# A linear-attention and squared-ReLU kernel: aligned tiles, a spread of u by a product, quarter products and a new order on every engine

## The chip, the cores and the metric

One core of a Trainium2 chip. The metric is the device time of one launch in microseconds; three runs of the kernel before gave 188.7, 190.06 and 193.52, with the median 190.06.

## The reference

Stage one is a linear attention with a per-channel decay w and a bonus u for the current token (batch 4, 8 heads, 768 tokens, 48 channels per head). Stage two is a feed-forward network with a squared ReLU on all 3072 tokens (384 to 2048 to 384).

```
state = 0                                   # per batch and head, 48 x 48
for t in range(768):
    cur  = outer(u * k[t], v[t])
    y[t] = r[t] @ (state + cur)
    state = w[t][:, None] * state + outer(k[t], v[t])
x = y with heads side by side               # 3072 x 384
out = maximum(x @ w_in, 0)**2 @ w_out
```

## The kernel before

The 3072 tokens are cut into twelve steps of 256, three to a batch. A step has two chunks c of 64 token pairs; the pair's two tokens are j = 0 and 1, so 128 partitions hold 128 pairs. One step s runs through these operations:

- `ld.s.w`, `.r`, `.k`, `.v` (L161): 384 KB each from HBM, descriptors of 384 bytes. The tiles of r and k have a third place per head, for the product with w.
- `ww_` (L243) multiplies the w of a pair, `lw_` (L247) takes the logarithm, `cum_` (L284 to L287) sums it over a chunk by products with triangular matrices, `exp_` and `ac_` (L291, L298) take the exponential. `rw_` and `kw_` (L256, L260) multiply r and k by w; `rd_` (L305) multiplies r and k by the decays into `rdec`.
- `tr_` with `rkt_`, or `dtr_` by DMA, transpose `rdec`. `p_` (L341) forms the scores in products of 64 rows by 64 columns of the array, four quarters of which work at once; `pm_` (L351, L354) masks them.
- `ku_`, `qp_`, `q_`, `vq_` (L264 to L277) form the bonus: u, k and r multiplied, summed over a head, times v.
- `su_` (L371) forms the change of the state, `ts_` and `sn_` (L381, L386) the next state S.
- `y_`, `yq_`, `yc_` (all recorded at L394) add up in one PSUM tile: masked scores times v, the bonus, and S. `ysb_`, `yt_`, `xt_` (L436, L444, L449), or `dyt_` by DMA, give xT.
- `m1_` (L464, eight per step, six products each) multiplies by w_in, `rl_` (L473 on ACT, L475 on DVE) applies the ReLU, `sq_` (L481, L483) squares, `m2_` (L489, eight per step, four products each) multiplies by w_out, `os_` (L496, L498) scales, `store` writes.

The weights come in eight blocks of 768 KB (`ld.g.i`, `ld.g.o`) and are cast to bf16 (`cast`, L184). `warm_` (L506) issues products of zeros that nothing uses.

Nothing is scheduled by a loop: the string `ORDER` lists every operation of the program, with the engine (`=A` ACT, `=V` DVE, `=G` POOL) and the PSUM place (`:0`, `:1`) where there is a choice, and a loop over its words issues them. Each engine runs its instructions in that order, and a load waits in the one queue of SP behind the loads and transposes before it. PSUM is split into two attention tiles of two banks (`att`), two banks for m1 (`m1_bank`) and two for m2 and the transposes (`bk`).

The bonus of a chunk has 64 rows (pairs) and must go to 128 output rows (both tokens j of a pair); `yq_` does that by a constant `spread` of 64 rows by 128 columns, zero in one half. u is brought to all 128 partitions by a load that reads its 1536 bytes 128 times (L189).

Of the kernel before, what the change touches and what calls it, by code (L numbers as in the profile page):

```python
# [17 lines left out]
ld.0.w warm_.16.0 ld.1.w ld.0.k ld.0.u ld.0.r ld.1.r ww_.1=V ww_.0=V ld.1.k ld.0.v lw_.0 lw_.1 kw_.0=V  # L18
cum_.1:0 ku_.0 cum_.0:1 ld.0.i warm_.13.0 ac_.0 ac_.1 rw_.0=V exp_.0 qp_.0 ld.1.v exp_.1 rd_.0.0 rd_.0.1
tr_.0.0:0 ld.1.i warm_.1.1 rw_.1=V ld.2.w rkt_.0.0=A tr_.0.1:1 q_.0 ku_.1 rkt_.0.1=A ld.3.i rd_.1.0  # L20
p_.0.0:mm v_.0=A kw_.1=V qp_.1 warm_.2.0 rd_.1.1 su_.0:1 ld.2.k tr_.1.0:0 pm_.0.0 ts_.0.0=A tr_.1.1:1
rkt_.1.0=A p_.0.1:0 sn_.0.0 ld.2.r pm_.0.1 rkt_.1.1=A vq_.0 v_.1=A ts_.0.1=V y_.0:0 q_.1 cast.i.0=A sn_.0.1
p_.1.1:mm yq_.0 pm_.1.1 yc_.0 vq_.1 p_.1.0:1 ysb_.0=A ld.2.i warm_.3.0 pm_.1.0 ld.0.o cast.i.1=A yt_.0:0
su_.1:0 xt_.0=V y_.1:1 ts_.1.0=V ld.1.o yq_.1 ww_.2=V m1_.0.2:0 sn_.1.0 m1_.0.3:1 rl_.0.2=A yc_.1 cast.i.3=V
rl_.0.3=A m1_.0.1:0 lw_.2 ts_.1.1=V ld.2.o ysb_.1=A m1_.0.6:1 sq_.0.1=V ld.2.v cum_.2:0 rl_.0.1=V rl_.0.6=A
yt_.1:1 exp_.2 m1_.0.7:1 xt_.1=V rw_.2=V m1_.0.0:0 rl_.0.7=A kw_.2=V rl_.0.0=A rd_.2.0 m1_.1.0:1 cast.i.2=G
ac_.2 m1_.1.7:0 sq_.0.3=A rl_.1.0=V tr_.2.0:0 rd_.2.1 ku_.2 ld.3.o rl_.1.7=A m1_.1.5:1 sq_.0.0=A ld.3.w
m1_.0.5:0 rl_.1.5=V ld.3.r tr_.2.1:1 cast.o.0=V sn_.1.1 rl_.0.5=A m1_.1.4:1 rkt_.2.0=V m1_.0.4:0 rl_.1.4=A
rkt_.2.1=A rl_.0.4=V qp_.2 m1_.1.1:1 sq_.1.2=V m2_.0.0.0:0 cast.o.1=A m1_.1.2:0 ld.3.k pp_.2:10 rl_.1.2=A
m2_.0.0.1 rl_.1.1=A pm_.2.1 v_.2=G sq_.0.2=A m1_.1.3:0 cast.o.2=G ld.3.v q_.2 m1_.1.6:1 m2_.0.1.0:1 pm_.2.0  # L30
rl_.1.6=A vq_.2 m2_.0.1.1 cast.o.3=A ld.4.w rl_.1.3=V su_.2:0 m2_.0.1.2 ww_.3=G sq_.1.0=A ld.4.r m2_.0.0.2
lw_.3 m2_.0.1.3 sq_.1.1=A cum_.3:1 os_.0.1=V ld.4.k m2_.0.0.3 rw_.3=V exp_.3 m2_.1.0.0:1 ts_.2.0=V kw_.3=G
sq_.1.3=A rd_.3.0 m2_.1.0.1 ld.5.r sn_.2.0 m2_.1.0.2 ac_.3 os_.0.0=A rd_.3.1 m2_.1.0.3 v_.3=A ku_.3
store.0.1 tr_.3.0:0 os_.1.0=V yy_.2:01 ww_.4=V qp_.3 ld.4.v rkt_.3.0=V lw_.4 tr_.3.1:1 ysb_.2=A m2_.1.1.0:0
rkt_.3.1=V ld.5.k ts_.3.0=A cum_.4:1 rw_.4=V sn_.3.0 yt_.2:1 exp_.4 m2_.1.1.1 xt_.2=V ac_.4 ld.5.w m2_.1.1.2
rd_.4.0 kw_.4=G m1_.2.1:1 ts_.3.1=V dtr_.4.0 ku_.4 m1_.2.0:0 rd_.4.1 rl_.2.1=A rl_.2.0=A m1_.2.5:1 q_.3
dtr_.4.1 pp_.3:01 sn_.3.1 rl_.2.5=A m1_.2.3:0 pm_.3.1 ld.6.w vq_.3 m2_.1.1.3 rl_.2.3=A pm_.3.0 m1_.2.2:1
v_.4=A qp_.4 m1_.2.6:0 ld.7.w sq_.2.0=A rl_.2.2=V yy_.3:10 rl_.2.6=V ld.5.v sq_.2.1=A ww_.5=V kw_.5=G
os_.1.1=A m1_.2.4:1 rw_.5=V ld.7.r ysb_.3=A m1_.2.7:0 lw_.5 yt_.3:1 ts_.4.0=V rl_.2.4=A m2_.2.0.0:0 ld.6.k
xt_.3=A sn_.4.0 sq_.2.2=V m2_.2.0.1 ku_.5 cum_.5:0 store.1.1 m2_.2.1.0:1 ac_.5 q_.4 exp_.5 m1_.3.1:1  # L40
ts_.4.1=V rl_.2.7=A m2_.2.1.1 rd_.5.0 rl_.3.1=A m1_.3.7:0 ww_.6=G sq_.2.3=A rd_.5.1 m2_.2.1.2 dtr_.5.0
sn_.4.1 rl_.3.7=A m1_.3.3:1 pp_.4:10 vq_.4 store.0.0 rl_.3.3=A m1_.3.2:0 dtr_.5.1 v_.5=A pm_.4.0 m1_.3.4:1
rl_.3.2=A ww_.7=G pm_.4.1 m2_.2.1.3 ld.6.r lw_.6 rl_.3.4=A qp_.5 m1_.3.0:0 ld.7.k lw_.7 kw_.6=V m2_.2.0.2
sq_.3.1=A ld.6.v yy_.4:10 ku_.6 ld.7.v rl_.3.0=V os_.2.1=V m2_.2.0.3 ysb_.4=A ts_.5.0=V store.1.0 sq_.3.0=V
m1_.3.5:1 sn_.5.0 yt_.4:1 rl_.3.5=A m1_.3.6:0 xt_.4=V sq_.3.2=A ld.8.w pp_.5:10 qp_.6 rl_.3.6=V m1_.4.0:1
os_.2.0=A pm_.5.0 sq_.3.3=A m2_.3.1.0:1 ld.8.r pm_.5.1 m1_.4.5:0 rw_.6=G rl_.4.0=A m2_.3.0.0:0 rw_.7=G q_.5
cum_.6:1 m1_.4.3:1 exp_.6 rl_.4.5=V kw_.7=G m2_.3.1.1 ac_.6 rd_.6.0 rl_.4.3=A cum_.7:0 vq_.5 m1_.4.1:0
exp_.7 rd_.6.1 dtr_.6.0 m2_.3.0.1 ac_.7 rd_.7.0 ww_.8=G v_.6=A m1_.4.2:1 dtr_.6.1 m2_.3.0.2 rd_.7.1
rl_.4.1=A v_.7=G rl_.4.2=A m2_.3.0.3 q_.6 sq_.4.0=A ld.8.k yy_.5:10 vq_.6 sq_.4.1=A m1_.4.4:0 ts_.6.0=A
dtr_.7.0 os_.3.0=A m1_.4.6:1 sn_.6.0 ysb_.5=A m2_.3.1.2 ld.9.r rl_.4.6=V ku_.7 lw_.8 yt_.5:0 store.2.0  # L50
rl_.4.4=A ts_.6.1=V m2_.3.1.3 xt_.5=V ld.9.w pp_.6:01 ld.9.k sn_.6.1 m1_.4.7:1 pm_.6.0 m1_.5.1:0 ku_.8
# [38 lines left out]
def kernel(  # L90
# [54 lines left out]
    def bf16_bank(i):  # L145
        return bk[int(i)][:].bitcast(BF16)
# [420 lines left out]
```

## Time and profile before

| | |
|---|---|
| Runs of the kernel before | 188.7, 190.06, 193.52 us |
| Span of the profiled execution, first to last instruction | 186.7 us |
| Its own total time | not on the page; the span is 2.0 under the fastest run, 3.4 under the median |
| Granted TensorE clock | 0.999 |
| Busy: PE, DVE, ACT, POOL | 177.0, 125.8, 125.1, 104.9 us |
| Chain that ended last | PE 80%, DVE 8%, ACT 5%, issue 3%, DMA 3% |
| DMA of the kernel | 35.46 MB, 82.5% of the sixteen engines' time |

How to read it. Busy time is the union of an engine's instructions. Idle time of an engine that is not the bound costs nothing. In the slices of the page a digit is the busy share in tenths of one fortieth of the span, 4.67 us. A timeline row gives start, length, engine, line, operation, output and inputs, the count of merged instructions, and in brackets the idle time before it with what ended it. A waits row gives the waiting engine and line, what it waited for, and total us, times and longest wait. A group row ends with the busy time, the mean ns of one, and the idle time before them. A chain row gives start, length and count. A row of the stretches gives the stretch, its length, busy time and count of an engine, the granted clock, the share of DMA engines busy and GB/s. PE's ends are modelled, so the time that a product costs is read from one start to the next.

### The profile page before, as it was taken

Reading aid. Unit: us, or ns where it says so; the run is one execution under the profiler, and the core shown is the slowest. Engines: PE = TensorE matmul, PEld = TensorE weight load, DVE = VectorE, ACT = ScalarE, POOL = GpSimd, SP = SyncE. Lnnn points to the kernel's source line nnn. Section 1 sums busy time; section 2 is a strip of 40 time slices with the busy share of each in tenths; the row PEclk is TensorE's granted clock in tenths of the full one; section 3 lists DMA queues with packets and bytes.
Section 4 is the critical chain, followed back from the end, with each engine's and each line's share of the span. In section 5 each row is a group of like instructions: output and inputs, shape, how many; then the busy total and the mean of one; then the engine's idle time right before and its main releaser. Section 6 shows DMA issues by size and latency. Waiting matters only on the chain.

```text
span 186.7 us, 5422 instructions
## 1 busy us (share of the span) xinstructions
PE 177.0 (95%) x2303; PEld 125.4 (67%) x2303; DVE 125.8 (67%) x170; ACT 125.1 (67%) x205; POOL 104.9 (56%) x99
## 2 busy tenths in 40 slices
PE   7686998999999999999999999999999999999992
PEld 2344587766777777777776766777666777776761
DVE  4379979686799876983849699795946472562020
ACT  5278978889659795797687577968541656156732
POOL 7289627695897998959496981563934130000000
PEclk9999999999999999999999999999999999999999
DMA  6999999999999999979999999890539150203022
GB/s 151 269 274 341 330 280 381 340 280 264 275 234 218 257 239 236 248 148 147 279 185 260 220 270 251 240 147 32 66 63 201 30 172 0 46 0 126 4 84 84
DMA packets 78952, 35.81 MB, mean 192 GB/s; under 512 B 72144, under 2 KB 77392, under 8 KB 78928
## 3 DMA queue, kind: packets, MB, share of 16 engines
q1 hardware_dynamic: 78928, 35.46, 82.5%
q8 instruction: 18, 0.29, 0.7%
q14 instruction: 6, 0.05, 0.1%
HBM read 25.36 MB, written 4.72 MB: 161 GB/s over the span
## 4 chain that ended last, share of the span: by engine, by line
PE 80%; DVE 8%; ACT 5%; issue 3%; DMA 3%; SPq 0%; ACTq 0%
PE m L464 32%; PE bk L489 31%; PE att L394 8%; DVE rdec_buf L305 4%; PE att L341 3%; PE att L371 3%; DMA w_raw<-in_w_dram 3%; PE bk L444 1%; PE att L286 1%; PE att L287 1%; ACT att L291 1%; DVE r_raw L256 1%; ACT ac_buf L298 1%; DVE pmT L351 1%; DVE pmT L354 1%
## 5 line engine op out<-in xcount | busy, mean ns | idle before, releaser
L464 PE MATMUL m<-xT,wi_sb 128*128 128x256 bf16 x576 | 74.3, 273 | 0.5 <-ACT gt L473 0.5
L489 PE MATMUL bk<-wo_sb,gt 128*128 128x384 bf16 x384 | 71.9, 326 | 0.0
L464 PEld LDWEIGHTS <-wi_sb 128*128 128x128 bf16 x576 | 54.9, 98 | 13.9 <-issue 1.4
L473 ACT ACTIVATE gt<-m 128x512 f16<-128x512 f32 x68 | 39.7, 596 | 34.4 <-PE m L464 34.1
L489 PEld LDWEIGHTS <-gt 128*128 128x128 bf16 x384 | 36.9, 98 | 19.3
L481 ACT ACTIVATE gt<-gt 128x1024 bf16<-128x1024 f16 x36 | 37.6, 1053 | 0.9 <-DVE gt L475 0.7
L354 DVE TENSOR_TENSOR pmT<-att,mask 128x1024 bf16<-128x1024 f32 x22 | 26.3, 1218 | 5.6 <-PE att L341 5.5
L386 POOL TENSOR_TENSOR S<-t_state,ac_buf 128x384 bf16<-128x384 f32 x20 | 18.7, 935 | 19.9 <-DVE t_state L381 13.2
L475 DVE TENSOR_SCALAR gt<-m 128x512 f16<-128x512 f32 x28 | 19.2, 687 | 14.6 <-PE m L464 11.9
L264 POOL TENSOR_TENSOR ku<-k_raw,u_bc 128x768 f32<-128x768 f32 x12 | 22.5, 1878 | 9.1 <-DVE q L273 4.7
L269 POOL TENSOR_TENSOR ku<-ku,r_raw 128x768 f32<-128x768 f32 x12 | 22.9, 1910 | 1.0 <-DMA r_raw<-in_r_dram 0.8
L277 POOL TENSOR_TENSOR vq<-v_raw,q 128x768 bf16<-128x768 f32 x12 | 18.2, 1520 | 9.1 <-DVE q L273 4.8
L305 DVE TENSOR_TENSOR rdec_buf<-r_raw,att 128x768 bf16<-128x768 f32 x12 | 11.3, 952 | 3.8 <-ACT att L291 2.2
L498 DVE TENSOR_SCALAR o_sb<-bk 128x384 f32<-128x384 f32 x11 | 6.1, 551 | 11.0 <-PE bk L489 11.0
L291 ACT ACTIVATE att<-att 128x768 f32<-128x768 f32 x12 | 9.4, 795 | 3.7 <-PE att L287 3.6
L305 DVE TENSOR_TENSOR rdec_buf<-k_raw,att 128x768 bf16<-128x768 f32 x12 | 11.4, 947 | 0.5 <-ACT ac_buf L298 0.5
L506 PE MATMUL bk<-warm 128*128 128x512 bf16 x35 | 10.5, 452 | 1.2 <-DVE half_ones L212 1.2
L273 DVE TENSOR_REDUCE q<-ku 128x16 f32<-128x768 f32 x12 | 11.3, 943 | 0.0
L496 ACT ACTIVATE o_sb<-bk 128x384 f32<-128x384 f32 x13 | 6.4, 490 | 6.2 <-PE bk L489 6.2
L483 DVE TENSOR_TENSOR gt<-gt 128x1024 bf16<-128x1024 f16 x12 | 8.9, 753 | 2.0 <-ACT gt L473 2.0
L381 DVE TENSOR_TENSOR t_state<-S,att 128x384 f32<-128x384 bf16 x16 | 8.7, 546 | 1.8 <-PE att L371 1.8
L247 ACT ACTIVATE lw_buf<-ww 128x384 bf16<-128x384 f32 x12 | 6.2, 524 | 5.3 <-DVE ww L243 5.3
(72 smaller groups left out, 179.8 us busy)
## 6 DMA issues: line engine op xcount, KB each, us to landing
w_raw<-in_w_dram SPq DMA_DIRECT2D x12, 384.0 KB, 5.1
k_raw<-in_k_dram SPq DMA_DIRECT2D x12, 384.0 KB, 6.1
r_raw<-in_r_dram SPq DMA_DIRECT2D x12, 384.0 KB, 6.2
v_raw<-in_v_dram SPq DMA_DIRECT2D x12, 384.0 KB, 6.0
out_dram<-o_sb SPq DMA_DIRECT2D x24, 192.0 KB, 3.1
w_st<-in_moe_w_in_dram SPq DMA_DIRECT2D x4, 768.0 KB, 8.5
w_st<-in_moe_w_out_dram SPq DMA_DIRECT2D x4, 768.0 KB, 8.7
rkT<-rdec_buf SPq DMA_TRANSPOSE x16, 4.0
```

The costliest lines, as they stand in the source:

```text
L264: nc.gpsimd.tensor_mul(ku[:], raw["k", s][:, :, 1:3, :], u_bc[:, :, None, :].to_broadcast([C, H, 2, D]))
L269: nc.gpsimd.tensor_mul(ku[:], ku[:], raw["r", s][:, :, 0:2, :])
L277: nc.gpsimd.tensor_mul(vq[:].rearrange("p j h d -> p h j d"), raw["v", s][:], tiles.pop(("q", s))[:, :, :, None].to_broadcast([C, H, 2, D]))
L305: nc.vector.tensor_mul(rdec[:, i, :, :, 0:D], x.rearrange("p h j d -> p j h d"), cs[:, i, 0:DM].rearrange("p (h d) -> p h d", h=H)[:, None ...
L354: nc.vector.tensor_mul(pmT, ps_p[:].rearrange("p e (a x) -> p (e a) x", a=2), mk.to_broadcast([C, 4, 2 * C]))
L386: nc.gpsimd.tensor_mul(t[:], tiles.pop(("ts", s, c))[:].rearrange("p (a e d) -> p a e d", a=HP, e=2), tiles["a_c", s][:, :, c, :, None].to ...
L394: nc.tensor.matmul(ps_y[rows, c, cols], lhsT, rhs, start=fresh, stop=True, skip_group_check=True)
L464: nc.tensor.matmul(ps1[:, j, :], wi_sb[:, n // 4, kk, n % 4 * 128:(n % 4 + 1) * 128], tiles["xT", s][:, :, kk, :], start=(kk == 0), stop=( ...
L473: nc.scalar.activation(rl, m1, AF.Relu, scale=RS)
L475: nc.vector.tensor_scalar(out=rl, in0=m1, scalar1=RS, scalar2=0.0, op0=ALU.mult, op1=ALU.max)
L481: nc.scalar.activation(gt, rl, AF.Square)
L489: nc.tensor.matmul(m2, gt[:, n, c * C:(c + 1) * C], wo_sb[:, n, :], start=(n == 0), stop=(n == NT - 1))
```

## The change

- Tiles: all buffers are allocated once, each a multiple of 128 bytes long, and handed out by a small allocator (`buf`). r and k get 160 elements of room per head instead of 144, with the place that a load writes on a multiple of 128 bytes. Output tiles reuse one weight buffer.
- PSUM: the four banks of m1, m2 and the transposes become one pool (`one`), any of which an operation may name.
- u: one row of 1536 bytes is loaded, an f32 product with a row of ones spreads it over the partitions (`ub_`), and ACT copies it out (`uc_`).
- The bonus: `spread` goes; `yq_` multiplies by 64 x 64 blocks of the identity into the two halves of the output rows, four products on four quarters of the array.
- The order: `pp_` and `yy_`, which kept p, and su, y, yq and yc, together, are taken apart, and the whole string is another one, with other engines for many operations. Casts of w_in: all four on ACT (two before). ReLU: 51 on ACT and 45 on DVE (68 and 28). Products ww, rw, kw: 25 on POOL and 11 on DVE (15 and 21). Dummy products: 24 (35). The number of m1, m2, attention operations and transposes by DMA is the same.

```diff
-ld.0.w warm_.16.0 ld.1.w ld.0.k ld.0.u ld.0.r ld.1.r ww_.1=V ww_.0=V ld.1.k ld.0.v lw_.0 lw_.1 kw_.0=V
-cum_.1:0 ku_.0 cum_.0:1 ld.0.i warm_.13.0 ac_.0 ac_.1 rw_.0=V exp_.0 qp_.0 ld.1.v exp_.1 rd_.0.0 rd_.0.1
...
+ld.0.w ww_.0=V ld.1.w ld.0.u ld.0.r ld.0.k ld.1.k rw_.0=G warm_.10.1 lw_.0 ww_.1=V lw_.1 kw_.0=V cum_.0:1 exp_.0 ac_.0
+rd_.0.0 ub_:1 uc_=A warm_.1.3 cum_.1:0 ld.1.r ld.0.v ld.0.i warm_.4.3 tr_.0.0:0 rd_.0.1 tr_.0.1:1 ku_.0 ac_.1 ld.1.v
+exp_.1 warm_.4.2 rkt_.0.0=A kw_.1=V rd_.1.1 ld.1.i ld.2.i rkt_.0.1=A v_.0=A rw_.1=G warm_.1.0 p_.0.0:n rd_.1.0 su_.0:1
+ld.3.i tr_.1.1:2 ts_.0.0=A qp_.0 sn_.0.0 ld.2.w ld.2.k pm_.0.0 q_.0 p_.0.1:0 vq_.0 ku_.1 warm_.4.0 pm_.0.1 tr_.1.0:3
+rkt_.1.0=V rkt_.1.1=A cast.i.0=A ld.2.r ld.2.v ld.0.o y_.0:0 yc_.0 yq_.0 v_.1=A ld.3.k ts_.0.1=V sn_.0.1 p_.1.1:n
+pm_.1.1 ysb_.0=A p_.1.0:1 yt_.0:3 xt_.0=V su_.1:0 m1_.0.1:3 qp_.1 ts_.1.0=V sn_.1.0 cast.i.1=A pm_.1.0 cast.i.2=A
...
+        w=(4, [C, H, 2, D], FP32), r=(4, [C, 1280], FP32), k=(4, [C, 1312], FP32), v=(4, [C, H, 2, D], FP32),
...
+    for kind, first in (("r", 0), ("k", 16)):
+        free[kind] = [t[:, first:first + H * 160].rearrange("p (h x) -> p h x", h=H)[:, :, 0:3 * D].rearrange(
+            "p h (n d) -> p h n d", n=3) for t in free[kind]]
...
     def load_u():
-        nc.sync.dma_start(
-            out=u_bc[:],
-            in_=bass.AP(tensor=u.tensor, offset=u.offset,
-                        ap=[[0, C]] + [list(x) for x in u.ap]))
+        nc.sync.dma_start(out=u_row[0:1, :],
+                          in_=bass.AP(tensor=u.tensor, offset=u.offset, ap=[[0, 1]] + [list(x) for x in u.ap]))
+
+    def ub_():
+        tiles["ub"] = one[int(slot["ub_",])]
+        nc.tensor.matmul(tiles["ub"][:, 0:DM], ones_row[0:1, :], u_row[0:1, :], start=True, stop=True)
+
+    def uc_():
+        copy = nc.scalar.copy if where["uc_",] == "A" else nc.vector.tensor_copy
+        copy(u_bc[:].rearrange("p h d -> p (h d)"), tiles["ub"][:, 0:DM])
...
     def yq_(s):
-        vq = tiles.pop(("vq", s))
-        for j in range(2):
-            for c in range(2):
-                part = slice(c * Q, (c + 1) * Q)
-                y_mm(s, c, slice(0, DM), spread[part, j], vq[part, j].rearrange("p h d -> p (h d)"))
+        vq = buf("vq", s)
+        for c in range(2):
+            part = slice(c * Q, (c + 1) * Q)
+            for j in range(2):
+                y_mm(s, c, slice(0, DM), ident[part, part], vq[part, j].rearrange("p h d -> p (h d)"), j)
...
-    def yy_(s):
-        if s + 1 < NS:
-            su_(s + 1)
-        y_(s)
-        yq_(s)
-        yc_(s)
```

More of the change, by code (lines that the diff above doesn't have):

```diff
@@ L23 @@
[L23 to L27, printed above, removed]
@@ new lines @@
+    att = [ps_pool.tile([C, 2, 512], FP32, name=f"att{i}") for i in range(2)]
+    one = [ps_pool.tile([C, 512], FP32, name=f"one{i}") for i in range(4)]
+    def bf16_bank(i):
+        return one[i][:].bitcast(BF16)
+    kinds = dict(
+        w=(4, [C, H, 2, D], FP32), r=(4, [C, 1280], FP32), k=(4, [C, 1312], FP32), v=(4, [C, H, 2, D], FP32),
+        w_st=(4, [C, 4 * DM], FP32), ww=(2, [C, H, D], FP32), v_bf=(3, [C, H, 2, D], BF16),
+        ku=(2, [C, H, 2, D], FP32), q=(3, [C, 32], FP32), vq=(2, [C, 2, H, D], BF16), vqt=(2, [C, 2, DM], BF16),
+        rkT=(2, [C, 2, 2, HP, C], BF16), pmT=(2, [C, 2, 4, 2, C], BF16), t=(2, [C, DM], FP32),
+        S=(6, [C, HP, 2, D], BF16), y_sb=(2, [C, 2, DM], BF16), xT=(4, [C, 2, KT, C], BF16),
+        gt=(3, [C, NT, T], BF16))
@@ new lines, with uses_of, buf @@
+    uses = dict(w=4, r=4, k=4, v=3, w_st=2, ww=2, v_bf=3, ku=3, q=2, vq=2, vqt=2, rkT=5, pmT=3, t=2, y_sb=2,
+                xT=9, gt=20, o=2)
+    live, done = {}, {}
+    def uses_of(kind, key):
+        if kind == "S":
+            s, c = key
+            return 2 if c and s % NB == NB - 1 else 3
+        return uses[kind]
+    def buf(kind, *key):
+        held = live.setdefault((kind,) + key, [])
+        if not held:
+            held += [free[kind].pop(0), uses_of(kind, key)]
+        held[1] -= 1
+        if not held[1]:
+            given = live.pop((kind,) + key)[0]
+            free[kind].append(given)
+            done[kind] = done.get(kind, 0) + 1
+            if kind == "w_st" and done[kind] == 5:
+                free["o"] += [given[:, i * DM:(i + 1) * DM] for i in range(4)]
+        return held[0]
@@ L199 @@
     ident = consts.tile([C, C], BF16)
-    spread = consts.tile([C, 2, C], BF16)
-    half_ones = consts.tile([C, 2], BF16)
+    half_ones = consts.tile([C, 64], BF16, name="half_ones")[:, 0:2]
     mask = consts.tile([C, 2, 2, Q], BF16)
@@ L256, in rw_ @@
-        mul(raw["r", s][:, :, 2, :], raw["r", s][:, :, 1, :], raw["w", s][:, :, 0, :])
+        r_raw, w_raw = buf("r", s), buf("w", s)
+        product("rw_", s)(r_raw[:, :, 2, :], r_raw[:, :, 1, :], w_raw[:, :, 0, :])
     def kw_(s):
-        mul = nc.gpsimd.tensor_mul if where["kw_", s] == "G" else nc.vector.tensor_mul
-        mul(raw["k", s][:, :, 0, :], raw["k", s][:, :, 1, :], raw["w", s][:, :, 1, :])
+        k_raw, w_raw = buf("k", s), buf("w", s)
+        product("kw_", s)(k_raw[:, :, 0, :], k_raw[:, :, 1, :], w_raw[:, :, 1, :])
@@ L400, in y_ @@
         tiles["y", s] = att[int(slot["y_", s])]
-        pmT, v_bf = tiles.pop(("pmT", s)), tiles["v", s]
+        pmT, v_bf = buf("pmT", s), buf("v_bf", s)
         for e in range(2):
@@ L535 @@
             where[(name,) + args] = engine
-            slot.update(zip(takes(name, *args), banks))
+            if bank:
+                slot[(name,) + args[:2]] = bank
             operations[name](*args)
```

315 lines of the change are left out of this document (142 added, 173 removed).

## The prediction

> **What bounds the kernel now.** I read the page's totals and slices first, then the waits, then the chain that ended last.
>
> ```profile
> span 186.7 us, 5422 instructions
> PE 177.0 (95%) x2303; PEld 125.4 (67%) x2303; DVE 125.8 (67%) x170; ACT 125.1 (67%) x205; POOL 104.9 (56%) x99
> PE   7686998999999999999999999999999999999992
> DMA  6999999999999999979999999890539150203022
> GB/s 151 269 274 341 330 280 381 340 280 264 275 234 218 257 239 236 248 148 147 279 185 260 220 270 251 240 147 32 66 63 201 30 172 0 46 0 126 4 84 84
> ```
>
> PE is full from the sixth slice (4.67 us each) to the last. The waits say who waits for whom:
>
> ```profile
> ACT gt L473 <- PE m L464: 34.1, 32, 4.0
> ...
> PE m L464 <- ACT gt L473: 0.5, 1, 0.5
> ```
>
> ACT's ReLUs wait 34.1 us for PE's products, PE waits 0.5 for the ReLUs. So the time is a prologue, then PE's own work, then a tail. The timeline of PE gives the prologue's end, the chain the tail:
>
> ```profile
> 1.19 5.73 PE L506 MATMUL bk<-warm 128*128 128x512 bf16 x16 [1.19 <-DVE half_ones L212]
> 9.20 2.97 PE L506 MATMUL bk<-warm 128*128 128x512 bf16 x13
> 14.70 0.42 PE L341 MATMUL m<-rkT 64*64 64x128 bf16 x16 [1.15 <-ACT rkT L323]
> 18.90 0.57 PE L394 MATMUL att<-v_bf,pmT 64*128 64x48 bf16 x32 [1.36 <-DVE pmT L354]
> 23.39 1.48 PE L464 MATMUL m<-xT,wi_sb 128*128 128x256 bf16 x12
> ...
> 177.50 5.86 PE bk L489 x36
> 183.39 0.49 ACT o_sb L496
> ```
>
> The first product with w_in starts at 23.4; PE ends at 183.4; the last scaling and store take 3.3. The 160 us between shrink only with PE's work or its waits. The page gives this execution's span, not its total: the three runs have a median of 190.06, 3.4 above the span, and a fastest of 188.7, 2.0 above. I make the sum on the span and carry the difference to the median.
>
> **The prologue.** Loads come from one queue, in order, so the next question is when each lands. The timelines of DVE and POOL show it, as the start of a job that waited for a load:
>
> ```profile
> 6.22 1.03 DVE L243 TENSOR_TENSOR ww<-w_raw 128x384 f32<-128x384 f32 x2 [2.59 <-DMA w_raw<-in_w_dram]
> 7.62 0.56 DVE L260 TENSOR_TENSOR k_raw<-k_raw,w_raw 128x384 f32<-128x384 f32 x1 [0.36 <-DMA k_raw<-in_k_dram]
> ...
> 11.05 0.95 DVE L305 TENSOR_TENSOR rdec_buf<-r_raw,att 128x768 bf16<-128x768 f32 x1 [0.34 <-ACT att L291]
> ...
> 16.44 1.28 DVE L351 TENSOR_TENSOR pmT<-m,mask 128x512 bf16<-128x512 f32 x2
> 17.64 1.21 DVE L354 TENSOR_TENSOR pmT<-att,mask 128x1024 bf16<-128x1024 f32 x1
> 13.20 1.82 POOL L264 TENSOR_TENSOR ku<-k_raw,u_bc 128x768 f32<-128x768 f32 x1 [0.81 <-DMA k_raw<-in_k_dram]
> ```
>
> From 6.2 (w of step 1) to 13.2 (k of step 1) four tensors of 384 KB and the 192 KB of u land: 7.0 us, about 1.5 per tensor. In the new order k of step 0 stands behind w, w, a u of one row and r, so it lands near 6.2 + 2 x 1.5 = 9.2. Then kw_ 0.56, and rd_0.0 starts at 9.8 where it started at 11.05. From rd_0.0 to the first score product took 3.65 (11.05 to 14.70): 13.45. DVE now does kw_1, rd_1.1 and rd_1.0 before the first mask product; r of step 1 lands at 12.2, its product on POOL ends at 13.2, rd_1.0 at 14.2. Then pm_0.0 1.28, q_0 0.94, pm_0.1 1.21: y_0 at 17.7 instead of 18.90. y_0 to yq_0 takes about 1.2 (18.9). ACT is free for the copy after v of step 1, which lands at 6.2 + 5 x 1.5 + 3.0 + 1.5 = 18.2 (one weight block is two tensors long) and takes 0.83: 19.0. The copy 0.8, the six transposes and their latency 0.55, the copy of xT 0.56 follow:
>
> ```profile
> 20.89 0.79 ACT L436 CAST y_sb<-att 128x768 bf16<-128x768 f32 x1
> 21.73 0.51 PE L444 MATMUL bk<-ident,y_sb 128*128 128x128 bf16 x6
> 22.42 0.55 DVE L449 COPY xT<-bk 128x768 bf16<-128x768 bf16 x1
> ```
>
> That gives a first product with w_in at 21.0: **-2.4 us**. Of before, 0.9 went because a cast of w_in stood ahead of this copy on ACT and three dummy products ahead of the transposes; both are moved. In exchange y_1 and its bonus, before the first product with w_in until now, come after it: **+0.8**.
>
> **Tiles at 128 bytes** have no row of their own: nothing here loads the same shape into an aligned and an unaligned place. Bounds: nothing, or all loads at the best slice's 381 GB/s instead of the 304 that slices 2 to 5 average, 20% of the 15 us of loads up to v of step 1: -3.0. Loads pace everything up to 21 us, and the addresses of all loaded tiles move, from 32 bytes past a multiple of 128 to 0; I take a third, **-1.0**. The one-row u takes 191 KB off the queue (already in the 9.2), and adds one f32 product and one copy of 128x384 on ACT (0.49, as the scaling at 183.39 above), in the time in which both wait for k.
>
> **The bonus on quarters.** The timeline of one step, and pieces of the chain:
>
> ```profile
> 135.73 0.49 PE L464 MATMUL m<-xT,wi_sb 128*128 128x256 bf16 x3
> 136.15 0.52 PE L371 MATMUL att<-v_bf,rdec_buf 64*128 64x96 bf16 x16
> 136.50 0.56 PE L394 MATMUL att<-v_bf,pmT 64*128 64x48 bf16 x32
> 136.91 0.48 PE L394 MATMUL att<-vq,spread 64*128 64x384 bf16 x4
> 137.32 0.36 PE L394 MATMUL att<-S,rkT 128*64 128x96 bf16 x8
> ...
> 52.44 1.31 PE m L464 x12
> ...
> 54.59 0.57 PE att L341 x32
> ...
> 55.92 0.65 PE bk L489 x4
> ```
>
> A product of 384 columns is 0.65/4 = 0.163. The four of the bonus take 0.41 (136.91 to 137.32): two pairs, 0.325, and 0.09 for changing the array from 64x128 to 128x64. The same 0.09 shows where L464 gives way to L371: 0.42 (135.73 to 136.15) for three of 1.31/12 = 0.109. Four quarters at once cost 0.163 at best; by the score products, where 32 quarters of 128 columns take 0.57 (some three at a time), 0.21. With the change behind them that is 0.25 to 0.30: 0.11 to 0.16 saved, over twelve steps 1.3 to 1.9. But the quarters are a fourth shape between two others, and su, y, yq and yc no longer stand together. Counted in the two programs, PE changes shape 67 times before and 81 after: 14 x 0.09 = 1.3 given back. Net **-0.3** (-0.9 if a change between two 64-row shapes costs nothing, +0.6 if it costs double).
>
> The Trainium skill (TensorEngine Tiling (Array Packing), Tiling Modes, Key Properties) says that changing the tiling mode drains TensorE while changing the tile alone doesn't; the 0.09 above agrees, and by that rule the quarters pay only where the shape before or after them is the same.
>
> **The orders.** ReLUs move from ACT (68 to 51) to DVE (28 to 45), and products with w from DVE (21 to 11) to POOL (15 to 25):
>
> ```profile
> L473 ACT ACTIVATE gt<-m 128x512 f16<-128x512 f32 x68 | 39.7, 596 | 34.4 <-PE m L464 34.1
> L475 DVE TENSOR_SCALAR gt<-m 128x512 f16<-128x512 f32 x28 | 19.2, 687 | 14.6 <-PE m L464 11.9 <-ACT gt L473 2.6
> L243 POOL TENSOR_TENSOR ww<-w_raw 128x384 f32<-128x384 f32 x5 | 5.0, 1007 | 0.6 <-DMA w_raw<-in_w_dram 0.6
> ```
>
> ACT loses 17 x 0.6 = 10 us, DVE gains 11.7 and loses about 10 products of 0.55 or more, POOL gains 10 x 1.0. All stay off the bound by the 34.1 and 11.9 in which they wait for PE; cover gone, POOL is the one with a price (below). The products with w_in get four banks in place of two, so the bank waits of PE (0.5 in the waits) should go: **-0.4**; other waits I take as many as before.
>
> **Sum:** -2.4 + 0.8 - 1.0 - 0.3 - 0.4 = -3.3: span 183.4, time 190.06 - 3.3 = 186.8, 1.7% less. (2% either way, 3.8 us, is about what a measurement of this kernel can tell from no change.)
>
> **Rivals.** *The lead is kept and the loads gain their full bound:* -1.0 becomes -3.0, time 184.8, faster by over 2%. For it: DMA is at 9 in every slice up to the 18th, and weights are still landing when PE begins. Against: only the prologue turns loads into time. With the better shape bound (-0.6 more) and a product with w_in at 20.5 it is 183.7; PE's work allows no less.
>
> *POOL becomes the bound of steps 3 and 4 (slower).* PE takes its queue in order, so yq_3 blocks all behind it until vq_3 is there. In the POOL and PE timelines and POOL's busy time by stage:
>
> ```profile
> 29.30 1.46 POOL L184 CAST wi_sb<-w_st 128x1536 bf16<-128x1536 f32 x1 [4.72 <-DMA w_st<-in_moe_w_in_dram]
> 55.39 1.48 POOL L277 TENSOR_TENSOR vq<-v_raw,q 128x768 bf16<-128x768 f32 x1 [0.24 <-PE att L341]
> 58.57 0.48 PE L394 MATMUL att<-vq,spread 64*128 64x384 bf16 x4
> 8.00:50.00 42.00, 30.31 (x21) 1.00 1.13 308
> ```
>
> vq_3 ends 1.7 us before PE wants it. After, seven more products of 1.0 stand ahead of it (the two casts remain, of other blocks), and PE comes about 2.4 sooner: POOL must win 7.0 + 2.4 - 1.7 = 7.7. It idled 11.7 of the 42 us from 8 to 50, of which 4.7 for one weight block that it no longer casts; so I expect it to win most. If it wins none, 186.8 + 7.7 = 194.5; it turns the sign once over 3.3 is lost, and passes 2% slower near 7.
>
> *Nothing is kept:* the products with w_in start sooner but stand waiting for casts or ReLUs, as ACT now casts all four blocks of w_in; the lead of 2.6 goes, time about 189.5.
>
> *The clock.* Dummy products fall from 35 to 24. The later thirteen took 2.97, 0.23 each; the first sixteen took 5.73, 2.1 more than at that rate: PE starts slow, although the granted clock reads 1.00. If it falls back once while it waits for loads, the real products lose as much: time 188.9. For: the first dummies stop near 5.5 now. Against: the thirteen at 9.20 were fast though the sixteen had ended at 6.92.
>
> The Trainium skill (TensorE: Matmul & The Clock Gate, Part 1) halves the clock after an idle window of about 3.4 us; no gap in the walk above is that long, so by that rule the clock stays.
>
> **How the numbers follow.** Forecast near 186.8 0.38; loads or quarters better, 183 to 186, 0.32; nothing kept or the clock, 188.5 to 192, 0.16; POOL, 192 to 196, 0.14. The forecast stands so close to 2% (186.3) that a third of it counts as faster: faster 0.32 + 0.13 = 0.45; slower takes the POOL case and 0.04 of the third, 0.18; within 2% 0.37. Range 182.8 to 192.0: below it lies PE's work, above it most of the POOL case.
>
> **What would show it.** Right: first product with w_in near 21 us, k of step 0 landed near 9 us; PE's end 158 to 160 us after that start; the bonus at 0.2 per step, with 0.09 ahead of it; POOL with little idle time from 30 to 65 us and no wait of PE for vq. Wrong: a first product at 23 or later, tensors still 1.5 us apart, or waits of PE for vq_3, casts or ReLUs of over 2 us together.

## The result, and the profile after

The changed kernel takes 183.08 us (median of four runs, 182.77 to 183.29), the kernel before 189.47 (188.7 to 193.52); the ratio is 0.968, with a 95% interval of 0.9635 to 0.9725. The profiled execution took 183.09, its span is 181.3. The forecast was 186.8, 1.7% faster; it is 3.2% faster, inside the range and 0.6 below the lowest time that the first rival allowed. One of the four runs before, 193.52, was a slow one: without it the median before is 188.88. So the 6.4 us between the medians is more than the change is worth: it is 5.8 without that run, 5.3 to 5.5 against the later sessions (188.41 to 188.6), and 5.4 by the spans of the two profiles (186.7 and 181.3).

The page of the changed kernel (totals and slices, here 4.53 us each), and its waits, in the form in which those of before were shown:

```profile
span 181.3 us, 5434 instructions
PE 174.1 (96%) x2293; PEld 125.1 (69%) x2294; DVE 127.1 (70%) x176; ACT 120.0 (66%) x191; POOL 110.8 (61%) x104
PE   7978899999999999999999999999999999999992
DMA  5999999998999599979999559983659821302023
...
ACT gt_b L481 <- PE one L474: 24.0, 17, 4.9
...
PE one L474 <- ACT gt_b L481: 0.5, 1, 0.5
```

PE is still the bound: its slices stand at 9 from the sixth to the last but one. The timeline of PE, and the last piece of the chain:

```profile
1.19 4.45 PE L513 MATMUL one<-warm 128*128 128x512 bf16 x10 [1.19 <-DVE warm L235]
15.86 0.57 PE L411 MATMUL att<-v_bf_b,pmT_b 64*128 64x48 bf16 x32 [0.29 <-DVE pmT_b L376]
17.96 0.51 PE L457 MATMUL one<-ident,y_sb_b 128*128 128x128 bf16 x6 [0.50 <-ACT y_sb_b L449]
19.12 2.78 PE L474 MATMUL one<-xT_b,wi_sb 128*128 128x256 bf16 x24 [0.20 <-DVE xT_b L461]
22.43 0.81 PE L474 MATMUL one<-xT_b,wi_sb 128*128 128x256 bf16 x6 [0.53 <-ACT gt_b L481]
...
168.90 9.11 PE one L497 x56
```

The first product with w_in starts at 19.12 (before 23.39): 4.3 sooner. PE ends at 178.0 (before 183.4). So 158.9 us lie between, 1.1 less than the 160 of before. The loads show why the start is early. DVE's and POOL's jobs that waited for a load:

```profile
4.23 0.56 DVE L267 TENSOR_TENSOR ww_b<-w_b 128x384 f32<-128x384 f32 x1 [0.48 <-DMA w_b<-in_w_dram]
5.44 0.56 DVE L267 TENSOR_TENSOR ww_b<-w_b 128x384 f32<-128x384 f32 x1 [0.66 <-DMA w_b<-in_w_dram]
7.89 0.56 DVE L283 TENSOR_TENSOR k_b<-k_b,w_b 128x384 f32<-128x384 f32 x1 [1.89 <-DMA k_b<-in_k_dram]
10.40 1.10 POOL L279 TENSOR_TENSOR r_b<-r_b,w_b 128x384 f32<-128x384 f32 x1 [0.24 <-DMA r_b<-in_r_dram]
```

From w of step 0 (4.2) to r of step 1 (10.4) lie five tensors (w, r, k, k, r): 1.2 us each, where before it was about 1.5. k of step 0 is there at 7.9; the prediction had 9.2.

### The profile page after: what moved, and what is told of

Read it like the earlier page. It is cut to its first block, busy times and chain, and to the rows that moved or that the text cites. A ratio compares the mean times of both kernels' runs of the same rounds, so it can differ in the third digit from the quotient of the medians.

```text
span 181.3 us, 5434 instructions
## 1 busy us (share of the span) xinstructions
PE 174.1 (96%) x2293; PEld 125.1 (69%) x2294; DVE 127.1 (70%) x176; ACT 120.0 (66%) x191; POOL 110.8 (61%) x104
## 4 chain that ended last, share of the span: by engine, by line
PE 86%; DMA 5%; SPq 5%; issue 1%; ACT 1%
PE one L497 35%; PE one L474 34%; PE att L411 7%; DMA w_st_b<-in_moe_w_in_dram 5%; SPq L180 3%; PE att L365 3%; PE att L387 2%; SPq L188 1%; PE one L341 1%; PE att L313 1%; PE one L457 1%; PE att L314 1%; SPq L208 1%; PE att L311 0%; ACT gt_b L481 0%
## 5 line engine op out<-in xcount | busy, mean ns | idle before, releaser
L474 PE MATMUL one<-xT_b,wi_sb 128*128 128x256 bf16 x576 | 71.2, 273 | 0.7 <-ACT gt_b L481 0.5
L497 PE MATMUL one<-wo_sb,gt_b 128*128 128x384 bf16 x384 | 68.9, 326 | 0.0
L497 PEld LDWEIGHTS <-gt_b 128*128 128x128 bf16 x384 | 36.7, 98 | 21.7 <-ACT gt_b L489 0.2
L481 ACT ACTIVATE gt_b<-one 128x512 f16<-128x512 f32 x51 | 29.9, 596 | 24.6 <-PE one L474 24.0
L483 DVE TENSOR_SCALAR gt_b<-one 128x512 f16<-128x512 f32 x45 | 30.3, 685 | 17.0 <-PE one L474 15.7
L489 ACT ACTIVATE gt_b<-gt_b 128x1024 bf16<-128x1024 f16 x38 | 39.4, 1054 | 0.9 <-DVE gt_b L483 0.7
L376 DVE TENSOR_TENSOR pmT_b<-att,mask 128x1024 bf16<-128x1024 f32 x22 | 26.0, 1216 | 6.2 <-PE att L365 6.2
L286 POOL TENSOR_TENSOR ku_b<-k_b,u_bc 128x768 f32<-128x768 f32 x12 | 22.8, 1910 | 3.0 <-DMA k_b<-in_k_dram 2.3
L291 POOL TENSOR_TENSOR ku_b<-ku_b,r_b 128x768 f32<-128x768 f32 x12 | 21.8, 1814 | 1.2 <-DMA r_b<-in_r_dram 1.2
L297 POOL TENSOR_TENSOR vq_b<-v_b,q_b 128x768 bf16<-128x768 f32 x12 | 18.1, 1506 | 0.4 <-DVE q_b L294 0.3
```

What stands on the lines that cost most here:

```text
L286: nc.gpsimd.tensor_mul(buf("ku", s)[:], buf("k", s)[:, :, 1:3, :], u_bc[:, :, None, :].to_broadcast([C, H, 2, D]))
L291: nc.gpsimd.tensor_mul(ku[:], ku[:], buf("r", s)[:, :, 0:2, :])
L297: nc.gpsimd.tensor_mul(buf("vq", s)[:].rearrange("p j h d -> p h j d"), buf("v", s)[:], buf("q", s)[:, :, :, None].to_broadcast([C, H, 2, D]))
L376: nc.vector.tensor_mul(pmT, ps_p[:].rearrange("p e (a x) -> p (e a) x", a=2), mk.to_broadcast([C, 4, 2 * C]))
L474: nc.tensor.matmul(ps1[:, j, :], wi_sb[:, n // 4, kk, n % 4 * 128:(n % 4 + 1) * 128], xT[:, :, kk, :], start=(kk == 0), stop=(kk == KT - 1))
L481: nc.scalar.activation(rl, m1, AF.Relu, scale=RS)
```

## The experiments

Fourteen kernels were run. Times are medians; the ratio is to the kernel before in the same session, whose median was 188.4 to 189.5. "The start" is that of the first product with w_in.

### One part taken out at a time

**All tiles off the 128 bytes** (e1): one small tile ahead of all others shifts every address by 32 bytes.

```diff
+    shift = consts.tile([C, 8], FP32, name="shift")
     free = {kind: [consts.tile(shape, dtype, name=f"{kind}_b{i}") for i in range(n)]
...
```

> The changed kernel with every tile moved by 32 bytes, so that no tile starts at a multiple of 128 (as before the change); all else the same. Theory A (the loads land faster at aligned places, and this is the gain that the forecast undersized): tensors of 384 KB land 1.4 to 1.5 us apart instead of 1.2, k of step 0 at 8.7 to 9.3 instead of 7.87, the first product with w_in at 20.5 to 21.3 instead of 19.12, time 184.6 to 185.5. Theory B (the gain over the forecast comes from the order): first product within 0.3 of 19.12, time 183.0 to 183.5.

It took 187.34, ratio 0.9916 (0.9882 to 0.9949): 4.3 more than the changed kernel, so most of the gain is gone. One row of DVE, then the stretches of PE (stretch, its length, busy time, count, granted clock, DMA share, GB/s) and two of its waits, in this kernel:

```profile
8.93 0.56 DVE L284 TENSOR_TENSOR k_b<-k_b,w_b 128x384 f32<-128x384 f32 x1 [2.46 <-DMA k_b<-in_k_dram]
...
10.00:17.00 7.00, 6.29 (x80) 0.76 1.17 311
...
24.00:50.00 26.00, 25.36 (x347) 1.00 1.05 284
50.00:90.00 40.00, 38.58 (x584) 1.00 1.02 224
...
46.27 2.11 PE L498 MATMUL one<-wo_sb,gt_b 128*128 128x384 bf16 x12 [0.64 <-ACT wo_sb L201]
84.17 0.52 PE L388 MATMUL att<-v_bf_b,rdec_buf 64*128 64x96 bf16 x16 [1.08 <-ACT v_bf_b L276]
```

and the last two stretches in the changed kernel:

```profile
24.00:50.00 26.00, 26.00 (x324) 1.00 1.04 306
50.00:90.00 40.00, 40.00 (x644) 1.00 0.97 232
```

k of step 0 comes at 8.9, 1.0 later, and the start is 21.58, 2.5 later. A part of the 2.5 is the clock, which fell from 10 to 17 us (0.76); in e6 below, where k comes at 8.95 and the clock stays at 1.00, the start is 20.57. The other half of the loss is spread: between 24 and 90 us PE idles 2.06 us where the changed kernel idles not at all. Most of it (0.64 and 1.08) is for casts of weights and of v, which had waited for their loads.

**The old spread of the bonus** (e3): `spread` and its four products of 64 rows by 128 columns come back.

```diff
-                y_mm(s, c, slice(0, DM), ident[part, part], vq[part, j].rearrange("p h d -> p (h d)"), j)
+                y_mm(s, c, slice(0, DM), spread[part, j], vq[part, j].rearrange("p h d -> p (h d)"))
```

> The changed kernel with the old bonus: four products of 64 rows by 128 columns with the constant spread, in the place in the order where the quarters stand. By the forecast's prices: the four take 0.33 instead of 0.16 (twelve steps, +1.9), and the shape changes fall from 81 to 78 (-0.3): +1.6, time 184.7. Rival (shape changes eat the saving): within 0.5 of 183.1.

It took 184.32, ratio 0.9759 (0.971 to 0.9807): the quarters are worth 1.2 us. One step's bonus on PE and what follows it, with the spread:

```profile
67.33 0.50 PE L415 MATMUL att<-vq_b,spread 64*128 64x384 bf16 x4
67.76 0.42 PE L369 MATMUL att<-rkT_b 64*64 64x128 bf16 x16
```

and in the changed kernel:

```profile
67.02 0.36 PE L411 MATMUL att<-vq_b,ident 64*64 64x384 bf16 x4
67.20 0.39 PE L365 MATMUL att<-rkT_b 64*64 64x128 bf16 x16
```

From one start to the next it is 0.43 and 0.18. The four quarters run at the same time (0.16 was the best that the prediction allowed), and where score products follow, which have the same 64 by 64 shape, no change of shape is paid. Where a product with w_in follows in the changed kernel, it is 0.29 (24.14 to 24.43).

**All three parts out, only the order left** (e4): e1 and e3 together, and u read 128 times again, without `ub_` and `uc_`. The order keeps its engines and the pool of four banks.

> The changed kernel with the three other parts undone: tiles moved by 32 bytes, spread bonus, u loaded 128 times by DMA. What is left is the order with its engines and the pool of four banks. Theory A, by the prices above: 183.1 + 2.0 + 1.6 + 0.6 = 187.3, so the order alone is worth 1.5 to 2 of the 6. Theory B: below 186, so the order carries most of the gain.

It took 188.55, ratio 0.9986 (0.9964 to 1.0008): by itself the order is worth nothing that can be measured. The start was at 23.56, no better than before (23.39); k of step 0, behind two w, u and r in the queue, was late:

```profile
10.76 0.56 DVE L290 TENSOR_TENSOR k_b<-k_b,w_b 128x384 f32<-128x384 f32 x1 [4.41 <-DMA k_b<-in_k_dram]
```

PE idled 3.75 us behind it and the clock fell (0.86 from 10 to 14 us, 0.62 from 14 to 17); in all ten runs its mean was below 1 (0.982 to 0.991).

**u read 128 times, all else as in the changed kernel** (e7):

```diff
-... ub_:1 uc_=A ...
...
-        nc.sync.dma_start(out=u_row[0:1, :], ...ap=[[0, 1]] + ...
+        nc.sync.dma_start(out=u_bc[:], ...ap=[[0, C]] + ...
```

> The changed kernel with u loaded 128 times by DMA (192 KB) in place of the one row, the f32 product and the copy. Theory (the one row is worth the time on the queue that it saves, at 1.2 us per 384 KB): k of step 0 lands 0.6 to 1.0 later than 7.87, the first product with w_in 0.6 to 1.0 later than 19.12, time 183.7 to 184.2. Rival (PE's f32 product and ACT's copy cost what the queue saves): 183.1 or less.

It took 186.26, ratio 0.9883 (0.9858 to 0.9907): 3.2 more, where 0.6 to 1.1 was expected. To see whether any 192 KB in that place of the queue cost that much or only this load, e11 keeps the one row and puts 128 different rows of 1536 bytes ahead of it:

```diff
+        nc.sync.dma_start(out=spare[:], in_=moe_w_out[0:C, :])
         nc.sync.dma_start(out=u_row[0:1, :],
...
```

> The changed kernel, one row of u as there, and ahead of it in the queue 192 KB that nothing uses: 128 different rows of 1536 bytes of w_out, in place of the 128 reads of the same row. Theory (192 KB at the head cost their share of the queue, and reading one row 128 times is what made the 128-fold load of u dear): k of step 0 lands 0.6 to 0.9 later than 7.87, time 183.5 to 184. Rival (any 192 KB there cost as much as the 128-fold load of u): k of step 0 near 10.6, time 186.3.

It took 183.66, ratio 0.9727 (0.9689 to 0.9765). DVE's job that waits for k of step 0, first with u read 128 times and then with the other 192 KB:

```profile
10.66 0.56 DVE L285 TENSOR_TENSOR k_b<-k_b,w_b 128x384 f32<-128x384 f32 x1 [4.73 <-DMA k_b<-in_k_dram]
```

```profile
8.31 0.56 DVE L285 TENSOR_TENSOR k_b<-k_b,w_b 128x384 f32<-128x384 f32 x1 [2.38 <-DMA k_b<-in_k_dram]
```

The same bytes delay k by 0.4 (7.89 to 8.31) when they are different rows, and by 2.8 when they are one row read 128 times. Both kernels move about the same number of packets (78928 and 78930), so it isn't smaller pieces. It is the repeated row that is dear; what in the memory or the DMA engines makes it so, no run here shows. In e7 the delay also opened a gap of 4.08 us of PE, in which the clock fell (0.86 on average over the first 24 us, below); the start was 23.44, so not all of its 4.3 us is the late k.

```profile
0.00:24.00 24.00, 17.12 (x220) 0.86 0.92 273
```

### Which tiles, and where the time goes

**Only the tiles that loads write** (e5), by the same small tile ahead of them and another behind them, and **64 bytes instead of 32** (e6, all tiles):

> The changed kernel with only the tiles that loads write (w, r, k, v and the staging tiles of the weights) 32 bytes past a multiple of 128; every tile that only the engines touch stays aligned. Theory (the gain of alignment is the time of the loads): as with all tiles shifted, 187.3, tensors 1.45 to 1.5 us apart at the start, first product with w_in near 21.6. Rival (the engines read and write aligned tiles faster, or the loads matter but only as part): 183 to 185, tensors 1.2 us apart.

> The changed kernel with all tiles 64 bytes past a multiple of 128. Theory (a piece of 384 bytes costs more as soon as its place is not a multiple of 128): 187.3 as at 32 bytes, tensors 1.45 us apart. Rival (64 bytes are enough): 183.1, 1.2 us apart. Between: 185, 1.3 us apart.

e5 took 186.45 (ratio 0.99, 0.9874 to 0.9925), e6 187.29 (0.9939, 0.9904 to 0.9975). So 64 is as bad as 32; in both, the first tensors land 1.5 us apart. With only the loads' places shifted, 3.4 of the 4.3 us are lost; whether the 0.9 between e5 and e1 is more than the spread of their runs (186.38 to 187.22 and 186.42 to 188.56) stays open.

**Half of the buffers each.** The prediction said that only the prologue turns loads into time. Two of the four buffers of w, r, k and v are shifted: those that steps 0 and 1 use first (e9), or those of steps 2 and 3 (e10).

```diff
+            if kind in ("w", "r", "k", "v") and i == shifted[0]:
+                shift = consts.tile([C, 8], FP32, name=f"shift_{kind}")
             free[kind].append(consts.tile(shape, dtype, name=f"{kind}_b{i}"))
+            if kind in ("w", "r", "k", "v") and i == shifted[1]:
+                shift_back = consts.tile([C, 24], FP32, name=f"shift_back_{kind}")
...
```

> The changed kernel with two of the four buffers each of w, r, k and v (those of steps 0 and 1, used again by later steps) 32 bytes past a multiple of 128; the other two, and the weights, stay aligned. Theory (both halves of the load stream count: the prologue by its start, later steps by waits): first product with w_in at 21 to 21.7 as with all shifted, later PE waits of 1 us at most, time 185 to 186.5. Rival (alignment pays only in the prologue): all of the loss is here, 187.

> The changed kernel with the other two of the four buffers each of w, r, k and v (steps 2 and 3, and their later uses) 32 bytes past a multiple of 128; the prologue's loads stay aligned. Theory (the loads set the pace behind the prologue too): first product with w_in at 19.1 as in the changed kernel, but PE waits for loaded data later on, 1 to 2 us together, time 184.2 to 185.2. Rival (only the prologue turns loads into time, as the prediction said): no later waits, 183.1.

e9 took 185.08 (0.9802, 0.9758 to 0.9846), e10 185.01 (0.9797, 0.9745 to 0.9848): the losses are 2.0 and 1.9, and together nearly the 4.3. The stretches of PE in e9:

```profile
24.00:50.00 26.00, 25.77 (x354) 1.00 1.06 304
50.00:90.00 40.00, 39.95 (x595) 1.00 0.99 230
```

and in e10, with three rows of its timeline:

```profile
24.00:50.00 26.00, 25.27 (x313) 1.00 1.01 286
50.00:90.00 40.00, 39.34 (x590) 1.00 1.00 234
...
37.60 2.76 PE L504 MATMUL one<-wo_sb,gt_b 128*128 128x384 bf16 x16 [0.29 <-POOL wo_sb L207]
44.53 2.11 PE L504 MATMUL one<-wo_sb,gt_b 128*128 128x384 bf16 x12 [0.44 <-ACT wo_sb L207]
81.52 0.52 PE L394 MATMUL att<-v_bf_b,rdec_buf 64*128 64x96 bf16 x16 [0.66 <-ACT v_bf_b L282]
```

e9 starts late (20.58, with the clock at 1.00) and then idles 0.28 us; e10 starts on time (19.14) and then idles 1.39 us, at products that stand behind a load. This falsifies the prediction's sentence: the load stream sets the pace in two places, and half of the gain lies behind the prologue.

### The old order

**Aligned tiles alone in the kernel before** (e2): r and k at 160 elements per head, and the small tiles rounded up.

> The kernel before with its tiles alone put on multiples of 128 bytes (r and k with the wider room per head); order, bonus and u unchanged. Theory A: tensors land 1.2 us apart, the first product with w_in comes 1 to 2 us sooner than 23.39, time 187.0 to 188.0. Theory B: within 0.4 of the kernel before, because its order has other waits ahead of the first product.

It took 193.19, ratio 1.0224 (1.0171 to 1.0278): slower than before by 2%, though tensors landed 1.2 us apart. The start was 27.17. The first row below is of the kernel before, the other two are of e2:

```profile
10.16 0.56 DVE L256 TENSOR_TENSOR r_raw<-r_raw,w_raw 128x384 f32<-128x384 f32 x1 [1.99 <-DMA r_raw<-in_r_dram]
...
6.54 0.56 DVE L267 TENSOR_TENSOR k_raw<-k_raw,w_raw 128x384 f32<-128x384 f32 x1 [0.17 <-DMA k_raw<-in_k_dram]
10.00 1.00 DVE L263 TENSOR_TENSOR r_raw<-r_raw,w_raw 128x384 f32<-128x384 f32 x1 [2.91 <-DMA r_raw<-in_r_dram]
```

With aligned tiles k of step 0 came 1.1 sooner (6.54, before 7.62), but r of step 0, which here stands behind the 128 reads of u, no sooner than before. So the old order got no lead. That it even lost has other causes, of which the stretches of PE show one:

```profile
10.00:17.00 7.00, 4.29 (x63) 1.00 1.05 323
17.00:20.10 3.10, 1.23 (x29) 0.94 1.09 366
20.10:27.00 6.90, 6.25 (x136) 0.53 0.99 310
```

PE was busy for about half of 10 to 20 us, and then had half its clock for nearly 6.9 us, in which real products ran. **The same with three groups of dummy products where PE idled** (e8: `warm_.4.2` ahead of `p_.0.0`, `warm_.3.1` ahead of `tr_.1.1`, `warm_.5.0` ahead of `y_.0`) tests what that cost:

> The kernel before with aligned tiles as in the earlier run (193.2, the granted clock at half from 20.0 to 26.8 us), and three groups of dummy products (4, 3 and 5) put where PE idled between 13 and 20 us. Theory (alignment alone lost because PE idled enough for the clock to fall): the clock stays at full through 20 to 27 us, the first product with w_in at 21.5 to 23, time 186 to 187.5, faster than before. Rival (the old order can't use faster loads, clock or not): 189 or more. Second rival (the dummies only delay): first product after 23.4, time 189 to 190.

The clock stayed at 1.00 in every stretch, and yet it took 191.98, ratio 1.016 (1.0091 to 1.0229). By the medians holding the clock was worth 1.2 us, though the runs of e8 spread from 190.03 to 192.76; something else makes most of the loss. The theory expected 186 to 187.5. Two rows of DVE in e8, with the jobs of POOL beside them:

```profile
12.78 1.99 DVE L263 TENSOR_TENSOR r_raw<-r_raw,w_raw 128x384 f32<-128x384 f32 x1
30.50 2.16 DVE L267 TENSOR_TENSOR k_raw<-k_raw,w_raw 128x384 f32<-128x384 f32 x1
...
12.54 1.81 POOL L271 TENSOR_TENSOR ku<-k_raw,u_bc 128x768 f32<-128x768 f32 x1
30.13 2.12 POOL L271 TENSOR_TENSOR ku<-k_raw,u_bc 128x768 f32<-128x768 f32 x1
```

The same two products in the kernel before:

```profile
12.79 0.55 DVE L256 TENSOR_TENSOR r_raw<-r_raw,w_raw 128x384 f32<-128x384 f32 x1
28.49 0.55 DVE L260 TENSOR_TENSOR k_raw<-k_raw,w_raw 128x384 f32<-128x384 f32 x1
```

In e8 each ends 0.42 after the POOL job beside it (14.35 and 14.77; 32.25 and 32.66): DVE stood until POOL was done. In the kernel before, POOL's job of step 1 waited for k until 13.20, when DVE's product was nearly over; with aligned tiles k comes sooner, POOL starts at 12.54, and DVE loses 1.44. Exactly that much later are the masks, and the start (24.82, 1.43 after 23.39). The one of step 2 gives PE a wait of 1.74:

```profile
33.59 0.62 PE L321 MATMUL bk<-ident,rdec_buf 128*128 128x128 bf16 x8 [1.74 <-DVE rdec_buf L312]
```

The Trainium skill (SBUF — State Buffer, SBUF: two separate sides) says that DVE and GpSimd share a pair of ports as an exclusive lock that is held for a whole instruction, and that a DVE operation with two inputs in SBUF takes it against a GpSimd operation that reads SBUF; these rows agree. **Those products on POOL** (e13), as the new order has them, test it:

```diff
-rw_.1=V ... rw_.2=V ... kw_.2=V
+rw_.1=G ... rw_.2=G ... kw_.2=G
```

> The kernel before with aligned tiles and the extra dummy products (192.0 in the earlier run), and three words changed: the products rw_1, rw_2 and kw_2 go from DVE to POOL, as the new order has them. In the earlier run DVE's rw_1 took 1.99 us (0.55 in the kernel before) and kw_2 2.16, each ending with the POOL product beside it, and everything behind them came that much later. Theory (aligned loads brought POOL's products onto DVE's, and DVE stands still while POOL works on f32 in SBUF; the order's share of the change is to take these products off DVE): first product with w_in at 22.7 to 23.4 in place of 24.82, no wait of PE for rdec of step 2, time 187.5 to 189. Rival (the old order is late for another reason): first product at 24.5 or later, 191 to 192.

It took 188.33, ratio 0.9981 (0.9956 to 1.0007): by the medians three words are worth 3.65 us, and the wait of 1.74 is gone. The start came at 24.23, not at 22.7 to 23.4: kw_1, which stayed on DVE, now met POOL's ku_1:

```profile
14.83 1.23 DVE L267 TENSOR_TENSOR k_raw<-k_raw,w_raw 128x384 f32<-128x384 f32 x1
...
13.82 1.82 POOL L271 TENSOR_TENSOR ku<-k_raw,u_bc 128x768 f32<-128x768 f32 x1
```

So the total bears the theory out, and the start only in part. Without the loss the aligned old order is as fast as the kernel before, not faster: r of step 0 still came behind u's 128 reads, at 10.12.

### Two more on the changed kernel

**Few dummy products** (e14): `warm_.1.3`, `warm_.4.3`, `warm_.4.2`, `warm_.1.0` and `warm_.4.0` out.

> The changed kernel without five of its six groups of dummy products in the prologue; only the first ten stay. Theory (the granted clock falls when PE idles for much of a few us in the prologue, as with the aligned old order): half clock for 3.4 or 6.8 us somewhere from 9 to 25 us, first product with w_in later than 19.12 by up to 1, time 183.8 to 186. Rival (the remaining work keeps the clock; the dummies are for nothing): clock 1.0 throughout, 182.5 to 183.2.

It took 184.96, ratio 0.9781 (0.9726 to 0.9836). PE's timeline and stretches:

```profile
9.76 1.90 PE L341 MATMUL one<-ident,rdec_buf 128*128 128x128 bf16 x16 [2.39 <-DVE rdec_buf L332]
21.44 3.81 PE L474 MATMUL one<-xT_b,wi_sb 128*128 128x256 bf16 x30
...
0.00:10.00 10.00, 6.42 (x27) 0.93 0.92 245
10.00:17.00 7.00, 5.63 (x80) 0.50 1.06 343
17.00:24.00 7.00, 6.67 (x119) 0.63 1.03 337
```

The clock lost 0.07 of 10 us, 0.50 of 7 and 0.37 of 7, 6.8 us in all, so it stood at half for 13.6 us; the start is 2.3 later, and 1.9 us are lost. Three of the four runs have a mean clock of 0.961 and take 184.84 to 185.08, the fourth has 0.981 and takes 183.33. This is the fourth rival of the prediction, in a kernel without its cover. The longest idle time behind the first dummies was 2.39.

**ACT's third cast behind the first ReLU** (e12), to take away PE's wait of 0.53 at 22.43:

```diff
-pm_.1.0 cast.i.2=A ... rl_.0.1=A ld.2.o
+pm_.1.0 ... rl_.0.1=A cast.i.2=A ld.2.o
```

> The changed kernel with one word moved: ACT's cast of the third block of w_in behind the first ReLU in place of ahead of it. In the changed kernel that cast waits for its load, and PE waits 0.5 us at 22.43 for the ReLU that stands behind it. Theory (that wait is on the path): it goes, span and time fall by 0.4 to 0.5, to 182.6. Rival (the wait moves on: the next product with w_in needs that cast, or the next ReLU stands behind it): 183.0 to 183.4.

It took 183.18 (182.68 to 184.05), ratio 0.9707 (0.9671 to 0.9743): no gain. The wait moved, as the rival said; the second group of products needs what ACT now casts later:

```profile
21.11 2.85 PE L474 MATMUL one<-xT_b,wi_sb 128*128 128x256 bf16 x24 [0.86 <-ACT wi_sb L200]
```

## Why the prediction was right or wrong

The sum gave 3.3 us; it was 5.4 by the spans, on which the sum was made. Taken out one at a time, the alignment is worth 4.3 by the medians, u's one row 3.2, the quarters 1.2; all three out leave nothing. These add up to 8.7, more than the whole, because the alignment and the row need each other: without the row, k of step 0 comes at 10.7 in the aligned kernel (e7) and at 10.8 in the unaligned one (e4). In spans, everything but the alignment (e1) is worth 0.9, where the prediction had 2.3 (2.4 - 0.8 + 0.3 + 0.4), and the alignment 4.5 (185.8 to 181.3), where it had 1.0.

- **The bound: right.** PE is full between prologue and tail, and the spans differ by the start (4.3) and by what lies behind it (1.1).
- **Tiles at 128 bytes, -1.0: the step that failed.** Its bounds were 0 and -3.0, of which it took a third without a row that says why; against the full bound it held that "only the prologue turns loads into time". The loads are 20% faster per tensor (1.2 for 1.5), so the price per load was at the bound, not at a third of it. And of the 4.5 us, 2.46 are the start and 2.06 are waits from 24 to 90 us, where the argument had put nothing; e10 has 1.9 us of loss with the start kept. The row that spoke for the full bound stood in the prediction: DMA at 9 from the second slice to the 17th, at 7 in the 18th, and at 9 again to the 25th.
- **The prologue, -2.4: about right as a lead, but not kept.** k of step 0 was put at 9.2 without the alignment; e1 has 8.9. The start was put at 21.0; e1 has 21.58, and e6, whose clock stayed at 1.00, 20.57. But e1 is only 1.3 faster than the kernel before in its session (188.6), and the quarters alone are 1.2: the loads took the lead back as waits (2.06 us of idle PE from 24 to 90, 0.63 in the kernel before). The prediction took these other waits "as many as before". Only with aligned tiles is the lead kept.
- **u, "191 KB off the queue": mis-sized.** It was priced by its bytes, half of a tensor's 1.5 us. In the aligned kernel the repeated row holds k of step 0 back by 2.8. In the kernel before the price is not far off: r of step 0, the first load behind the row, comes 2.5 behind k of step 0 (7.62 and 10.16), 1.0 more than a tensor; with aligned tiles there (e2) it is 3.5, 2.3 more than a tensor. In the new order the repeated row costs k 1.8 with unaligned tiles (e4 against e1) and 2.8 with aligned ones. So its price rises where the loads are faster, which the prediction did not ask.
- **The quarters, -0.3: mis-sized.** The saving of 1.3 to 1.9 fits what is measured; but 14 more shape changes were charged to them. Counted in the programs, the kernel with the old spread (e3) has 78, the changed one 81: the quarters add three, at 0.09 each 0.3, which leaves 1.0 to 1.6; measured 1.2. The other eleven belong to the order and to u's product. The Trainium skill's rule that the prediction named (TensorEngine Tiling (Array Packing), Tiling Modes, Key Properties: a drain for a new mode, none for a new tile) agrees: 0.18 where score products follow, 0.29 where a product with w_in does.
- **y_1 ahead of or behind the start, +0.8, and four banks, -0.4: not measured apart.** Behind the start the change gained 1.1 us in all, nearly the 1.2 of the quarters; PE's one wait for a ReLU (0.53) is as long as before, so the four banks took no wait away. Whether y_1 cost its 0.8 there, and what paid for it, stays open.
- **The orders' engines, at nothing: wrong.** The cover was read from waits for PE, but the price was between DVE and POOL. With aligned loads, DVE's products beside POOL cost the old order 3.65 us. The new order has them on POOL; no run puts them back on DVE in the changed kernel, so what it owes to this is not shown.
- **Rivals.** The first, with the loads at their full bound, came closest (184.8, its floor 183.7). POOL did not become the bound: PE has no wait for vq. The clock stayed at 1.00 in the changed kernel, but fell in e1, e2, e4, e5, e7 and e14. By the rule of the Trainium skill that the prediction cited (TensorE: Matmul & The Clock Gate, Part 1), it falls after an idle window of about 3.4 us. The gaps of e4 (3.75) and e7 (4.08) agree; but in e14 it fell with a longest idle time of 2.39, and in e2 of about 1.4, with PE busy for half of the time. The measurement decides: thin work was enough, without a gap of that length.

## What to carry to other kernels

When a load gets faster, look up who starts sooner by it, and on which other engine's work that falls: the same alignment cost 2.2% in one kernel and gained 2.3% in another, whose order and load of u were different. A lead in the prologue is worth only what the load stream behind it lets be kept, so read the slices of DMA over the whole span before calling loads a matter of the prologue. Read a small broadcast once and spread it on the chip: here one row read 128 times held the loads behind it up by 2.8 us, longer than two aligned tensors of 384 KB take.

## What the runs showed of the hardware that was not expected

- Loads in pieces of 384 bytes: 1.2 us per 384 KB where the place in SBUF is a multiple of 128 bytes, about 1.5 at 32 or 64 bytes past one (e1, e5, e6).
- 192 KB ahead of r and k of step 0 delayed k by 0.4 as 128 different rows (e11), by 2.8 as one row read 128 times (e7).
- A DVE product of two f32 tiles of 128x384 takes 0.55 alone and up to 2.16 beside a POOL job, ending 0.42 after it (e8, e13).
- The clock fell to half for about 3.4 us (e1), 6.8 (e2) and 13.6 (e14) in prologues without an idle time of 3 us. With the same longest idle time of 1.7 it fell in e1 and e5 and not in e6; what decides between them is open.
